# One query tile per head pair: transposes move from TensorE to VectorE blocks and transfers

## The chip, the cores and the metric

The kernel runs on one core of a Trainium2 chip. The metric is the device time of one execution in microseconds (us). All arithmetic of the reference is done on the core; the host only lays the inputs out and reads the result back.

## The reference

Attention with pooled queries, and two feed-forward layers behind it, all in float32.

```python
q_pool = q.reshape(B, H, S // 2, 2, D).mean(axis=3)          # B=2, H=8, S=1152, D=64
scores = q_pool @ k.T / sqrt(D)                              # 576 x 1152 for each head
attn = exp(scores - max) / (sum + 1e-9)
x = (attn @ v)  as (1152 tokens, 512)
x = softplus(x @ w_in) @ w_out                               # 512 -> 2048 -> 512
xn = x / rms(x) * rms_g
out = (silu(xn @ w_gate) * (xn @ w_val)) @ w_out2            # 512 -> 1536 -> 512
```

## The kernel before, in words

The 16 heads are taken as 8 pairs (`pb` 0 to 7). The 576 pooled queries of a pair are four tiles of 128 (`x` 0 to 3) and a half tile (`x` = 4) in which the 64 queries of both heads lie side by side.

For a tile and a head, `qk` (L644) multiplies queries with keys into a score bank of PSUM (128 queries by 1152 keys, six matmuls), and `softmax` (L671) finds the row maximum on VectorE (DVE, `nm`, L677) and the exponentials on ScalarE (ACT, `p`, L679). The exponentials have queries on the partitions; the product with the values needs keys there. So `flip` (L687) transposes them on TensorE (PE) against an identity, 128x128 at a time (L698): nine blocks for each head, eighteen for a tile, in five groups (4, 4, 4, 4 and 2 blocks), each of which is copied from PSUM to the SBUF tile `pt` by ACT (L318) or DVE (L320). `av` (L713) then multiplies `pt` with the values (L723, 36 matmuls) and the result is copied to `O`. When a pair is complete, `scales` (L730) makes the reciprocals of the sums, sends them through DRAM (`row`, `rdb`), and `shift` (L776) multiplies `O` by them into the homes of the attention results (`X1`), from which `arrived` prepares the operands of the first layer.

Score banks: one for each head. `p`: two buffers for each head. `pt`: two. Transposed groups and `av` share two PSUM banks `t`. Values `v` and rounded keys `kk`: one set for even and one for odd pairs.

In the main loop the PE work of a full tile x is, in this order: the first group of tile x (head A), `qk` of tile x+1 head A, the second group, `av` of the tile before, the third and fourth groups (head B), `qk` of tile x+1 head B, the last group. PE follows that order as written. For ACT, DVE, GpSimd (POOL) and the two queues that issue transfers (SP, ACTQ), the class `Plan` writes the order: each operation has engines on which it can run with an estimated duration, a latest time worked out backward from the end, and the planner places ready operations by these. On the chip each engine then runs its list in order and waits at each entry for what that entry needs.

SBUF is cut into areas (`AREAS`); `alloc` gives out columns of an area, prefers columns that no one has used, and makes a new owner wait for all operations of the old one. Beside attention, `decode` (L367) turns the weights of the first layer from 64-bit into 32-bit halves; four decodes are done during attention (`early`, L1115), each in a room of 2048 columns of area KF, whose 11330 columns also hold the homes `X1`. Two more are planned right after the attention loop, with rooms in KF or in LF; LF can be used only when attention's own tiles are done.

```python
T[0]()
qk(pb, x + 1, 0)
T[1]()
if prev:
    av(*prev)
if pb and x == 0:
    scales(pb - 1)
    shift(pb - 1)
T[2]()
T[3]()
if x < NF - 1:
    qk(pb, x + 1, 1)
T[4]()
```

Of the kernel before, what the change touches and what calls it, by code (L numbers as in the profile page):

```python
# [12 lines left out]
F32 = mybir.dt.float32  # L13
# [3 lines left out]
ALU = mybir.AluOpType  # L17
# [3 lines left out]
P = 128  # L21
B, H, S, D = 2, 8, 1152, 64
# [3 lines left out]
KC = DM // P  # L26
J1 = 2048 // P
J2 = 1536 // P
CK = S // P
NP = B * H // 2  # L30
NF = SQ // P
C = 2 * NF + 1
N = 384
# [2 lines left out]
AREAS = {"KF": 11330, "KR": 15360, "MR": 8760, "LR": 13632, "LF": 4608}  # L36
SEM = 0.1
SLACK = 1.0
WAIT = 3.5
WARM = 20  # L40
WAKE = 16
MM = N / 2400 + 0.014
# [17 lines left out]


class Op:
    __slots__ = ("fn", "opts", "lat", "deps", "after", "succ", "late", "n", "seq", "ready", "left", "start", "end", "eng")


class Plan:
# [64 lines left out]
        self.rings.setdefault((tag, bufs), []).append(b)  # L131
        return b

    def op(self, opts, fn, r=(), w=(), lat=0.0, after=()):
        o = Op()
        o.fn, o.opts, o.lat = fn, opts, lat
        o.deps, o.after, o.succ = set(), set(after), []
        o.n = len(self.ops)
        for keys, writes in ((r, False), (w, True)):
            for b, part in keys:  # L140
                assert b.live, "a freed buffer"
                o.deps |= self.before(b, part, writes)
        for keys, writes in ((r, False), (w, True)):
            for b, part in keys:
                (b.writers if writes else b.readers).setdefault(part, []).append(o)
                if not b.ops or b.ops[-1] is not o:
                    b.ops.append(o)
        o.deps.discard(o)
        self.ops.append(o)
        if opts[0][0] == "PE":  # L150
            self.pe.append(o)
        return o
# [9 lines left out]
    def order(self):  # L162
        for (tag, bufs), insts in self.rings.items():
            for x, b in enumerate(insts):
                if x >= bufs:
                    for o in b.ops:
                        o.deps.update(insts[x - bufs].ops)
                if x:
                    for o in b.ops:
                        o.after.add(insts[x - 1].ops[0])  # L170
        for b in self.placed:
            for o in b.ops:
                for p in b.prior:
                    for u in p.users:
                        o.deps.update(u.ops)
        for a, b in zip(self.pe, self.pe[1:]):
            b.after.add(a)
        for o in self.ops:
            o.deps.discard(o)
            o.after -= o.deps  # L180
            o.after.discard(o)
            o.left = len(o.deps) + len(o.after)
            for d in o.deps:
                d.succ.append((o, True))
            for d in o.after:
                d.succ.append((o, False))
        topo = [o for o in self.ops if o.left == 0]
        left = {o.n: o.left for o in self.ops}
        for o in topo:
            for s, _ in o.succ:  # L190
                left[s.n] -= 1
                if left[s.n] == 0:
                    topo.append(s)
        assert len(topo) == len(self.ops), [o.fn for o in self.ops if left[o.n]][:4]
        for o in reversed(topo):
            e, d = o.opts[0][:2]
            need = 0.0
            for s, hard in o.succ:
                if hard:
                    need = min(need, s.late - o.lat - (SEM if s.opts[0][0] != e else 0.0))  # L200
                elif e == "PE" == s.opts[0][0]:
                    need = min(need, s.late)
                else:
                    need = min(need, s.late + d)
            o.late = need - d
        self.span = -min(o.late for o in self.ops)
        return self.run()

# [64 lines left out]
def body(ctx: ExitStack, tc: tile.TileContext, kT, qT, v, w1, w1o, wg, wv, w2o, rg, outT):  # L273
    nc = tc.nc
    ctx.enter_context(tc.manual_schedule())
    engines = {"ACT": nc.scalar, "DVE": nc.vector, "POOL": nc.gpsimd}
    plan = Plan()
# [46 lines left out]

    issued = {"SP": [], "ACTQ": []}

    def load(out, src, kb, w, queue="SP", lat=2.2):
        q = nc.sync if queue == "SP" else nc.scalar
        o = op([(queue, 0.6 + max(0, kb / 220 - 0.6))], lambda e: q.dma_start(out=out(), in_=src), w=w, lat=lat,
               after=issued[queue][-1:] if len(issued[queue]) < 10 else ())  # L330
        issued[queue].append(o)
        return o
# [34 lines left out]
    def decode(srcs, combine, phase, fs, rs):  # L367
# [13 lines left out]
        def word(w, x0, x1):  # L381
            return raw()[:, x0:x1, :].rearrange("p x (f w) -> p x f w", w=2)[:, :, :, w]

        def each(t, x0, x1):
            return t()[:, x0 * DM:x1 * DM].rearrange("p (x f) -> p x f", f=DM)
# [32 lines left out]
        for w, t in ((1, b), (0, s)) if combine else ((1, b),):  # L418
            for x0, x1 in cuts:
                n = (x1 - x0) * DM  # L420
                rp = [(room, (w, x)) for x in range(x0, x1)]
                hp, lp = [(t.hi, x) for x in range(x0, x1)], [(t.lo, x) for x in range(x0, x1)]
                op([act(n)], lambda e, w=w, t=t, x0=x0, x1=x1: copy(
                    e, each(t.hi, x0, x1), word(w, x0, x1).bitcast(F32)), r=rp, w=hp)
                op([pool(n)] if phase == "exp" else [dve(n)], lambda e, w=w, t=t, x0=x0, x1=x1: tt(
                    e, each(t.lo, x0, x1), word(w, x0, x1).bitcast(F32), each(t.hi, x0, x1), ALU.subtract), r=rp + hp, w=lp)
        plan.free(room)

    class Operand:
# [110 lines left out]
    def prep(pb):  # L540
# [10 lines left out]
        def load_q(h, c, queues=("SP", "SP")):  # L551
            cut = slice(0, 2 * P) if c == 0 else slice(2 * P, 2 * SQ) if c == 1 else slice(0, 2 * SQ)
            for z in range(2):
                parts = [(qr[h], (x, z)) for x in range(2) if c in (x, None)]
                load(lambda z=z: qr[h]()[z * D:z * D + D, cut], qT[n + h][:, cut], (cut.stop - cut.start) // 4, parts, queues[z])

        for h in range(2):
            qr.append(ring("a", "p1", [P, 2 * SQ], F32, 2) if first and h else ring("e", "qr", [P, 2 * SQ]))
# [4 lines left out]
        if first:  # L563
            for c, cut, m in kcuts:
                load(lambda cut=cut: kr()[:, cut], pairs[:, cut], 192, [(kr, c)], "SP" if c else "ACTQ", (2.0, 3.1, 2.7)[c])
            load_q(1, 0)
        else:
            load(kr, pairs, 576, [(kr, None)])
        for h in range(2):
            load_q(h, 1 if first else None)  # L570
            vt = ring("ea"[pb % 2], f"v{h}{pb % 2}", [P, CK, D])
# [115 lines left out]
    def flip(pb, x, todo, halves=False):  # L687
# [19 lines left out]
        for i, j in cuts:  # L707
# [2 lines left out]
                                        t()[:, i * P:j * P].rearrange("p (c q) -> p c q", c=j - i)),  # L710
               r=[(t, None)], w=[(pt, hc) for hc in todo[i:j]])

    def av(pb, x):  # L713
        s = st[pb]
        pt = units[pb, x, 0]["pt"]
        t = tbank()
        n = P if x < NF else D

        def go(e):
            for c in range(CK):  # L720
                for h in range(2):
                    rhs = pt()[:, c, h, :] if x < NF else pt()[:, c, 0, h * D:h * D + D]
                    nc.tensor.matmul(t()[h * D:h * D + D, :n], lhsT=s["v"][h]()[:, c, :], rhs=rhs,  # L723
                                     start=(c == 0), stop=(c == CK - 1))
        op([("PE", 0.1 + CK * 0.24 * n / P)], go, r=[(pt, None), (s["v"][0], None), (s["v"][1], None)],
           w=[(t, None)])
        o = s["O"]
        op([dve(n, psum=True), act(n, False)], lambda e: copy(e, o()[:, x * P:x * P + n], t()[:, :n]), r=[(t, None)], w=[(o, x)])
# [385 lines left out]
    prep(1)  # L1114
    early = {(1, 0): [(first_pair, 0)], (3, 0): [(first_pair, 1)], (4, 0): [(first_out, 0)], (5, 0): [(first_out, 1)]}  # L1115
    prev = None
    for pb in range(NP):
        last = pb == NP - 1
        for x in range(NF + 1):
            if x == 1 and 0 < pb < NP - 1:  # L1120
                prep(pb + 1)
            for make, n in early.get((pb, x), ()):
                make(n, "exp", "KF", "KR")
            T = turn(pb, x)
            if x < NF:
                T[0]()
                qk(pb, x + 1, 0)
                T[1]()
                if prev:
                    av(*prev)  # L1130
                if pb and x == 0:
                    scales(pb - 1)
                    shift(pb - 1)
                T[2]()
                T[3]()
                if x < NF - 1:
                    qk(pb, x + 1, 1)
                T[4]()
            else:
                if not last:  # L1140
                    qk(pb + 1, 0, 0)
                T[0]()
                T[1]()
                if not last:
                    qk(pb + 1, 0, 1)
                else:
                    nb, ab, bb = make_banks(1)
                    m1_alone(0, nb)
                T[2]()
                av(*prev)  # L1150
                if last:
                    scales(pb)
            prev = (pb, x)
    op([("ACTQ", 0.6)], lambda e: nc.scalar.dma_start(out=rgs, in_=rg), after=[plan.pe[-1]])
    m1_alone(1, bb)
    av(*prev)
    spread(NP - 1, 0)
    spread(NP - 1, 1)
    Y = make_banks(0)
# [211 lines left out]
```

## Time and profile before

| | |
|---|---|
| median of 3 runs | 671.76 us (671.13 to 672.28) |
| the profiled execution | 670.88 us |
| its span, first to last instruction | 668.8 us |
| granted PE clock | full through the span |
| PE busy | 660.2 us, 99% |
| DVE, ACT, POOL busy | 72%, 59%, 19% |

The span is what the profile's rows divide up; some 2 us of the execution lie outside it. Attention fills it from the start to about 257 us, the first layer follows to about 460 us, the second runs to the end. A line such as L318, L320 or L323 is a helper's (copies, two-operand arithmetic), so its groups are told apart by the tiles they write and read.

### The profile page before, as it was taken

To read this page: it belongs to the slowest core of one execution; us is meant where nothing else is said; L and a number is where in the kernel's file an instruction comes from. 1 tells how busy PE (TensorE), PEld (TensorE's weight loads), DVE (VectorE), ACT (ScalarE), POOL (GpSimd) and SP (SyncE) were. 2 spreads that over 40 slices of the span, in tenths; PEclk is the share of its full clock that TensorE was granted. 3 is DMA by queue.
4 is the path that set the end of the run, shared out by engine and by line. 5 is a ranking of instruction groups with operands and counts; after the bars stand their busy time and mean duration, and the time that the engine had idled before them with its cause. 6 is when DMAs were issued, how large, how long until landed. Compare 5 with 4: busy or idle time off the path is not lost.

```text
span 668.8 us, 12191 instructions
## 1 busy us (share of the span) xinstructions
PE 660.2 (99%) x4947; PEld 636.8 (95%) x4947; DVE 483.3 (72%) x745; ACT 395.6 (59%) x655; POOL 130.0 (19%) x147
## 2 busy tenths in 40 slices
PE   8999999999999999999999999999999999999997
PEld 7999999999988989999999999999999999999997
DVE  8878778787777877888787566788878777752221
ACT  4988888878887775556645745456545432432231
POOL 0442634564442210000000102001011001020000
PEclk9999999999999999999999999999999999999999
DMA  7775334224240204312321130150333122101011
GB/s 194 241 211 153 104 86 119 54 83 114 84 125 1 82 2 162 113 62 107 126 84 42 64 127 2 63 189 1 127 113 139 57 71 94 33 1 48 0 48 48
DMA packets 20854, 59.77 MB, mean 89 GB/s; under 512 B 3839, under 2 KB 6206, under 8 KB 20798
## 3 DMA queue, kind: packets, MB, share of 16 engines
q1 hardware_dynamic: 20286, 58.63, 27.4%
q8 instruction: 39, 0.64, 0.4%
q10 hardware_dynamic: 512, 0.36, 0.2%
q14 instruction: 17, 0.14, 0.1%
HBM read 56.59 MB, written 2.39 MB: 88 GB/s over the span
## 4 chain that ended last, share of the span: by engine, by line
PE 93%; DVE 3%; issue 1%; ACT 1%; DMA 1%; POOL 0%; ACTq 0%; DVEq 0%; POOLq 0%
PE s L838 28%; PE s L663 11%; PE t L723 11%; PE t L698 10%; PE s L903 7%; PE s L905 7%; PE s L904 7%; PE t L838 6%; PE t L905 2%; PE t L903 2%; PE t L904 2%; PE t L1065 1%; DVE nm L677 1%; DMA kr<-in_kT_dram 1%; DVE kk L323 0%
## 5 line engine op out<-in xcount | busy, mean ns | idle before, releaser
L677 DVE TENSOR_REDUCE nm<-s 128x1 f32<-128x1152 f32 x72 | 97.7, 1357 | 21.4 <-PE s L663 21.0
L679 ACT ACTIVATE p<-s,nm 128x1152 f32<-128x1152 f32 x72 | 88.2, 1225 | 14.4 <-DVE nm L677 13.0
L698 PE MATMUL t<-ident,p 128*128 128x128 f32 x576 | 84.2, 278 | 2.3 <-ACT pt L318 1.0
L318 ACT COPY pt<-t 128x512 f32<-128x512 f32 (+2 forms) x131 | 67.1, 525 | 28.1 <-PE t L698 20.7
L723 PE MATMUL t<-pt,v 128*64 128x128 f32 (+1 forms) x1440 | 80.1, 265 | 0.0
L698 PEld LDWEIGHTS t<-ident,p 128*128 128x128 f32 x576 | 64.9, 140 | 14.6 <-issue 4.8
L723 PEld LDWEIGHTS t<-pt,v 128*64 128x64 f32 x1440 | 71.3, 137 | 7.2 <-issue 6.6
L318 ACT CAST areaLR<-areaKF 128x384 fp32r<-128x384 f32 (+2 forms) x50 | 39.1, 783 | 42.4 <-PE t L905 19.1
L318 ACT CAST areaKR<-areaKF 128x1024 fp32r<-128x1024 f32 (+3 forms) x49 | 39.0, 804 | 24.5 <-PE t L905 7.0
L838 PE MATMUL s<-areaLR,areaKR 128*128 128x384 f32 x206 | 49.9, 339 | 0.2 <-DVE areaLF L941 0.2
L838 PE MATMUL s<-areaLR 128*128 128x384 f32 x204 | 49.3, 337 | 0.0
L838 PE MATMUL s<-areaMR,areaKR 128*128 128x384 f32 x190 | 44.4, 337 | 0.4 <-DVE s L320 0.4
L323 POOL TENSOR_TENSOR kk<-kr,kk 64x384 fp32r<-64x384 f32 x40 | 39.4, 1008 | 26.9 <-ACT kk L318 15.9
L320 DVE COPY pt<-t 128x512 f32<-128x512 f32 (+2 forms) x53 | 34.1, 657 | 12.7 <-PE t L698 12.2
L838 PE MATMUL s<-areaMR,areaLR 128*128 128x384 f32 x184 | 42.1, 337 | 0.0
L401 DVE SCALAR_TENSOR_TENSOR areaKF<-areaKF 128x1024 int32<-128x1024 int32 (+1 forms) x35 | 39.4, 1127 | 1.3 <-ACT areaKF L390 0.9
L838 PEld LDWEIGHTS s<-areaLR,areaKR 128*128 128x128 f32 x206 | 37.2, 188 | 0.5 <-DVE areaLF L941 0.5
L390 ACT ACTIVATE areaKF<-areaKF 128x1024 f32<-128x1024 f32 (+1 forms) x35 | 36.7, 1048 | 0.9 <-DMA areaKF<-in_w_dram 0.9
L838 PEld LDWEIGHTS s<-areaLR 128*128 128x128 f32 x204 | 36.7, 188 | 0.0
L323 POOL TENSOR_TENSOR gl<-g,gh 128x384 fp32r<-128x384 f32 x8 | 8.2, 1030 | 143.0 <-ACT gh L318 101.0
L323 DVE TENSOR_TENSOR areaKF<-areaKF 128x256 f32<-128x256 f32 (+2 forms) x77 | 35.5, 485 | 0.8
L838 PEld LDWEIGHTS s<-areaMR,areaKR 128*128 128x128 f32 x190 | 34.0, 188 | 0.7 <-DVE s L320 0.7
(270 smaller groups left out, 1560.0 us busy)
## 6 DMA issues: line engine op xcount, KB each, us to landing
qr<-in_qT_dram SPq DMA_DIRECT2D x28, 288.0 KB, 4.5
areaKF<-in_w_dram SPq DMA_DIRECT2D x14, 512.0 KB, 6.0
areaKF<-in_w1o_dram SPq DMA_DIRECT2D x14, 512.0 KB, 3.7
areaKF<-in_w2o_dram SPq DMA_DIRECT2D x12, 512.0 KB, 3.5
areaKF<-in_wg_dram SPq DMA_DIRECT2D x11, 512.0 KB, 3.6
areaKF<-in_wv_dram SPq DMA_DIRECT2D x11, 512.0 KB
v<-in_v_dram SPq DMA_DIRECT2D x16, 288.0 KB, 3.1
kr<-in_kT_dram SPq DMA_DIRECT2D x7, 576.0 KB, 3.9
```

What stands on the lines that cost most here:

```text
L318: nc.scalar.copy(out, in_)
L323: engines[e].tensor_tensor(out=out, in0=in0, in1=in1, op=o)
L401: op([dve(n)], lambda e, x0=x0, x1=x1: nc.vector.scalar_tensor_tensor(out=word(1, x0, x1), in0=word(1, x0, x1), scalar=3, in1=word(0, x0, ...
L663: nc.tensor.matmul(sc()[:, c, :N], lhsT=q()[:, cut], rhs=k()[:, c * N:(c + 1) * N], start=(i == 0), stop=(i == len(todo) - 1))
L677: u["mx"] = op([dve(S, psum=True)], lambda e: nc.vector.tensor_reduce(out=nm(), in_=sc()[:, :, :N], axis=AX.XY, op=ALU.max, negate=True), ...
L679: o = op([("ACT", 1.42)], lambda e: nc.scalar.activation(out=pr(), in_=sc()[:, :, :N], func=AF.Exp, bias=nm(), accum_out=s["den"]()[:, col ...
L698: nc.tensor.transpose(t()[:, i * P:(i + 1) * P], pr[:, c * P:(c + 1) * P], ident)
L723: nc.tensor.matmul(t()[h * D:h * D + D, :n], lhsT=s["v"][h]()[:, c, :], rhs=rhs, start=(c == 0), stop=(c == CK - 1))
L838: nc.tensor.matmul(out, lhsT=a(k), rhs=b(k), start=start and k + i == 0, stop=stop and k + i == 3, skip_group_check=seeded)
L903: nc.tensor.matmul(o, lhsT=wh, rhs=gh(), start=first, stop=False)
L904: nc.tensor.matmul(o, lhsT=wh, rhs=gl(), start=False, stop=False)
L905: nc.tensor.matmul(o, lhsT=wl, rhs=gh(), start=False, stop=last)
```

## The change

One tile (x = 1) of the pairs 1 to 6 is no longer transposed on PE. In its place `stream` has DVE transpose the exponentials of each head in 32x32 blocks (one instruction of 128x1152 for a head) into a tile `turned`, and 16 transfers of 32 partitions by 576 floats (2304 bytes) each, all on SP, carry the blocks to the partitions where they belong, in a tile `moved`. `av` of such a tile is taken one pair later, in tile x = 2 of the next pair (for pair 6: in tile 1 of pair 7), reads `moved` with a strided pattern (four runs of 32 floats), and `shift` of the pair follows it there. `turned` and `moved` have one buffer each (2304 columns of area KF each, held until the end of attention). The homes `X1` (4608 columns) are given out before the loop. The latest times of some operations are set earlier: 5 us for the low halves of decodes during attention, 4 us for the loads of queries and keys (all but the first pair's).

```diff
+HURRY = 5.0
+EARLY = 4.0
+G = 32
+GW = 2 * CK * G
+STREAMED = {(pb, 1) for pb in range(1, NP - 1)}
...
-            o.late = need - d
+            o.late = need - d - o.hurry
...
                 op([pool(n)] if phase == "exp" else [dve(n)], lambda e, w=w, t=t, x0=x0, x1=x1: tt(
-                    e, each(t.lo, x0, x1), word(w, x0, x1).bitcast(F32), each(t.hi, x0, x1), ALU.subtract), r=rp + hp, w=lp)
+                    e, each(t.lo, x0, x1), word(w, x0, x1).bitcast(F32), each(t.hi, x0, x1), ALU.subtract), r=rp + hp, w=lp,
+                   hurry=HURRY if phase == "exp" else 0.0)
...
-            load(kr, pairs, 576, [(kr, None)])
+            load(kr, pairs, 576, [(kr, None)], hurry=EARLY)
...
+    def stream(pb, x):
+
+        turned, moved = rings["turned"](), rings["moved"]()
+        units[pb, x, 0]["pt"] = moved
+        for h in range(2):
+            pr = units[pb, x, h]["p"]
+            op([("DVE", 1.37, 1)], lambda e, h=h, pr=pr: nc.vector.transpose(
+                turned().rearrange("p (b h c j) -> p h c b j", b=P // G, h=2, j=G)[:, h],
+                pr().rearrange("p k (c b j) -> p (k c) b j", b=P // G, j=G)), r=[(pr, None)], w=[(turned, h)])
+        for b in range(P // G):
+            for a in range(P // G):
+                op([("SP", 0.62)], lambda e, a=a, b=b: nc.sync.dma_start(
+                    out=moved()[b * G:(b + 1) * G, a * GW:(a + 1) * GW], in_=turned()[a * G:(a + 1) * G, b * GW:(b + 1) * GW]),
+                   r=[(turned, 0), (turned, 1)], w=[(moved, (a, b))], lat=4.0)
...
-                    rhs = pt()[:, c, h, :] if x < NF else pt()[:, c, 0, h * D:h * D + D]
+                    if (pb, x) in STREAMED:
+                        rhs = pt().rearrange("p (b h c j) -> p h c b j", b=P // G, h=2, j=G)[:, h, c]
+                    else:
+                        rhs = pt()[:, c, h, :] if x < NF else pt()[:, c, 0, h * D:h * D + D]
...
+    late = []
+    X1.of("alone", KC * N)
+    for t in X1.two:
+        for k in range(2):
+            X1.of((k, t))
+    for tag in ("turned", "moved"):
+        rings[tag] = plan.around(tag, 2 * S, 1, "KF")
...
+            if (pb, x) in STREAMED:
+                stream(pb, x)
+                qk(pb, x + 1, 0)
+                av(*prev)
+                qk(pb, x + 1, 1)
+                prev = late.pop() if late else None
+                late.append((pb, x))
+                continue
...
                 if prev:
                     av(*prev)
+                    if prev in STREAMED:
+                        shift(pb - 1)
                 if pb and x == 0:
                     scales(pb - 1)
+                    if (pb - 1, 1) not in STREAMED:
+                        shift(pb - 1)
+                T[2]()
+                if x == 1 and late:
+                    av(*late.pop())
                     shift(pb - 1)
-                T[2]()
...
     av(*prev)
+    for tag in ("turned", "moved"):
+        for b in rings.pop(tag).bases:
+            plan.free(b)
```

## Rows read from the trace of the kernel before

**Rows 1.** The page: busy time and share of the span by engine.
```profile
PE 660.2 (99%) x4947; PEld 636.8 (95%) x4947; DVE 483.3 (72%) x745; ACT 395.6 (59%) x655; POOL 130.0 (19%) x147
```
**Rows 2.** Busy time by stretch: start:end, length, engines, PE clock, DMA share, GB/s.
```profile
20.00:50.00 30.00, 29.79 (x323) 27.45 (x325) 23.25 (x37) 25.48 (x41) 13.81 (x17) 1.00 0.75 223
...
140.00:170.00 30.00, 29.79 (x323) 27.28 (x321) 23.21 (x32) 24.77 (x46) 16.87 (x21) 1.00 0.35 99
...
260.00:275.00 15.00, 15.00 (x88) 15.00 (x87) 13.34 (x20) 10.87 (x17) 1.02 (x1) 1.00 0.65 238
```
**Rows 3.** The chain that ended last, 100 to 136 us: start, length, what.
```profile
104.24 1.20 PE t L723 x36
...
114.13 0.66 PE t L698 x6
114.78 1.05 PE s L663 x6
115.84 0.44 PE t L698 x4
116.27 2.12 PE t L723 x36
118.39 1.05 PE t L698 x8
119.44 1.05 PE s L663 x6
120.49 0.65 PE t L698 x6
...
134.37 1.20 PE t L723 x36
```
**Rows 4.** Timeline from 119.8 us, part of it: scores, maximum, exponentials, copies.
```profile
119.81 0.68 PE L663 MATMUL s<-kk,qlB 128*128 128x384 f32 x3
...
120.64 1.36 DVE L677 TENSOR_REDUCE nm<-s 128x1 f32<-128x1152 f32 x1
120.74 1.08 ACT L318 COPY pt<-t 128x256 f32<-128x256 f32 x2
...
122.04 1.23 ACT L679 ACTIVATE p<-s,nm 128x1152 f32<-128x1152 f32 x1 [0.22 <-DVE nm L677]
```
**Rows 5.** Groups by shape, 28 to 247 us: count, busy us, mean ns.
```profile
L318 ACT COPY pt<-t 128x512 f32<-128x512 f32 x91 | 52.3, 586 | 24.0 <-PE t L698 19.1 <-PE t L1065 2.8
...
L320 DVE COPY pt<-t 128x512 f32<-128x512 f32 x41 | 27.7, 689 | 9.9 <-PE t L698 9.6
...
L318 ACT COPY pt<-t 128x256 f32<-128x256 f32 x25 | 9.3, 372 | 2.3 <-PE t L698 1.3
...
L320 DVE CAST kh<-kr 128x1152 fp32r<-128x1152 f32 x5 | 3.8, 751 | 0.8 <-PE s L663 0.8
```
**Rows 6.** Line L723 alone, semaphore waits in PE's queue: ns min/median/max, first and last.
```profile
L723 PEldq EVENT_SEMAPHORE  x8: 51/51/51, 19.1 to 229.0; - x8
```
**Rows 7.** Timeline of SP, 109 to 140 us and 195 to 330 us, parts.
```profile
113.93 2.46 SPq L756 DMA_DIRECT2D rdb<-row  x4
...
132.28 0.35 SPq L329 DMA_DIRECT2D kr<-in_kT_dram  x1
...
226.71 1.06 SPq L329 DMA_DIRECT2D areaKF<-in_w_dram  x2
258.47 0.80 SPq L329 DMA_DIRECT2D areaLF<-in_w_dram  x2
```
**Rows 8.** Timeline of POOL and of PE, 195 to 260 us, parts.
```profile
235.06 1.31 POOL L323 TENSOR_TENSOR areaKR<-areaKF,areaKR 128x512 fp32r<-128x512 f32 x1 [2.80 <-ACT areaKR L318]
...
257.07 0.42 PE L903 MATMUL s<-gh,areaKR 128*128 128x384 f32 x1
```

More of the change, by code (lines that the diff above doesn't have):

```diff
@@ L62 @@
 class Op:
-    __slots__ = ("fn", "opts", "lat", "deps", "after", "succ", "late", "n", "seq", "ready", "left", "start", "end", "eng")
+    __slots__ = ("fn", "opts", "lat", "deps", "after", "succ", "late", "n", "seq", "ready", "left", "start", "end", "eng", "hurry")
 class Plan:
@@ L132, in ring, with op @@
         return b
-    def op(self, opts, fn, r=(), w=(), lat=0.0, after=()):
+    def op(self, opts, fn, r=(), w=(), lat=0.0, after=(), hurry=0.0):
         o = Op()
-        o.fn, o.opts, o.lat = fn, opts, lat
+        o.fn, o.opts, o.lat, o.hurry = fn, opts, lat, hurry
         o.deps, o.after, o.succ = set(), set(after), []
@@ L325, in body, with load @@
     issued = {"SP": [], "ACTQ": []}
-    def load(out, src, kb, w, queue="SP", lat=2.2):
+    def load(out, src, kb, w, queue="SP", lat=2.2, hurry=0.0):
         q = nc.sync if queue == "SP" else nc.scalar
-        o = op([(queue, 0.6 + max(0, kb / 220 - 0.6))], lambda e: q.dma_start(out=out(), in_=src), w=w, lat=lat,
+        o = op([(queue, 0.6 + max(0, kb / 220 - 0.6))], lambda e: q.dma_start(out=out(), in_=src), w=w, lat=lat, hurry=hurry,
                after=issued[queue][-1:] if len(issued[queue]) < 10 else ())
@@ L554, in load_q @@
                 parts = [(qr[h], (x, z)) for x in range(2) if c in (x, None)]
-                load(lambda z=z: qr[h]()[z * D:z * D + D, cut], qT[n + h][:, cut], (cut.stop - cut.start) // 4, parts, queues[z])
+                load(lambda z=z: qr[h]()[z * D:z * D + D, cut], qT[n + h][:, cut], (cut.stop - cut.start) // 4, parts, queues[z], hurry=0.0 if first else EARLY)
         for h in range(2):
```

## The prediction

> **What bounds the kernel now.** I read the engines' busy shares first: PE is busy for 660.2 of 668.8 us [rows 1], so almost no time is left in which PE waits, and a change pays only by what it takes from PE's list or costs by the waits it puts there. A busy PE can still hide a wait in a stage, so I read the stretches next: during attention PE is busy 29.79 of each 30 us while DVE and ACT have 23.2 and 24.8 us of work in the same 30 [rows 2]. Two engines that are busy four fifths each and never hold PE up are near their limit but not at it; the reader should keep both halves of that. Third, the chain of waits through one pair shows that attention's end is set by PE alone, piece after piece, in the order written in the loop [rows 3]. A full tile is the stretch from 114.13 to 120.49: transposes 0.66 + 0.44 + 1.05 = 2.15 us, scores 1.05 + 1.05 = 2.10 us, product with the values 2.12 us, together 6.37 us. A pair is the distance between two of its half-tile products, 134.37 - 104.24 = 30.1 us [rows 3].
>
> **What is removed.** In six tiles the eighteen transposes go: 6 x 2.15 = 12.9 us of PE's list [rows 3]. With them go four copies of 512 columns and one of 256: on ACT 4 x 0.586 + 0.372 = 2.72 us for a tile, on DVE at 0.689 somewhat more [rows 5].
>
> **What is added on DVE.** Two block transposes of 128x1152 a tile. The trace has no DVE transpose. From below: DVE casts 128x1152 in SBUF in 0.751 us [rows 5]. From above: twice the row maximum over 1152 elements, which takes 1.36 us [rows 4], so 2.7 us. I take 1.36 us, the same engine with as many float32 elements read once each; the fast cast is nearer in place (SBUF) but a block transpose is less like a copy. So 2.72 us for a tile, as much as the copies that went. For a pair DVE and ACT together then still have 23.2 + 24.8 = 48.0 us per 30, of which 60 were on offer; a pair shortens to 27.95 us, 55.9 on offer, so their joint share rises from 80% to 86%.
>
> The Trainium skill speaks against this edit: the page "VectorE: DVE Perf Modes", section "Rules for kernel authors", says to transpose 128x128 on TensorE if a PSUM destination will do, and its section "The three transpose paths" gives 311 ns for a 128x128 bf16 block transpose on DVE. An estimate from that page is 9 x 311 ns = 2.8 us for a head. No row here has the operation; by the page's figure the sum would come out beyond the slow rival below, at about 684 us.
>
> **Where PE can now wait.** The streamed tile leaves PE only scores, product, scores: 1.05 + 2.12 + 1.05 = 4.22 us [rows 3]. The question is whether the softmax of tile 2 keeps up. From the end of the scores (120.49 [rows 3]) maximum and exponentials end at 122.04 + 1.23 = 123.27 [rows 4], 2.78 us later when both engines are at hand; I add 0.05 for the hand-over and use 2.83.
> Head A of tile 2: between its scores and its first transposes PE has the product and head B's scores, 2.12 + 1.05 = 3.17 us. Slack 0.34 us.
> Head B: between its scores and its transposes stand 0.44 + 1.05 + 0.44 us and a product of 2.12 us, 4.05 us. Slack 1.22 us. In pair 1 there is no older product to put there, so 1.93 us stand against 2.83: a wait of 0.9 us, once.
> The product inside the streamed tile needs all copies of tile 0. Its last group is now followed by 1.05 us of scores only, where transposes stood as well (0.66, 0.44 more). A copy of 256 columns (0.37) fits if ACT or DVE is free; behind a maximum (1.36) or an exponential (1.23) it is about 0.7 us late [rows 4, 5].
> For these two tight places I take 0.3 us a tile, between nothing and about 1.0: 6 x 0.3 = 1.8 us.
>
> **Semaphores.** The product of a streamed tile waits for 16 transfers. In the trace the product's line shows one extra wait instruction of 51 ns in PE's queue for each of the 8 pairs [rows 6], where fresh values arrive. Bounds: nothing, if PE's queue runs ahead while scores are computed; 16 x 0.051 = 0.82 us a tile if it can't. I take half, 0.4: 6 x 0.4 = 2.4 us.
>
> **Strided reads of the product.** No row has them. Bounds: nothing, or the product doubled (2.12 us more). I take nothing: the matmuls still read each value once and in runs.
>
> **Transfers.** 16 x 32 x 2304 bytes are 1.2 MB a pair. PE was as busy in the stretch with a DMA share of 0.75 as in the one with 0.35 [rows 2], so I charge no contention. On SP an issue takes 0.35 to 2.46 / 4 = 0.6 us [rows 7], so 16 take 5.6 to 9.8 us of a pair of 28, and they can't start before the older product has released `moved`. Queued behind them on SP are the next loads of keys, queries and values, `row`, `rdb`, and decode loads. Keys for pair 5 are loaded at 132.28, about when pair 4 begins, a pair ahead of their use [rows 7]; 9.8 us late would still be in time. The cover is that pair-long lead; without it the 9.8 us would fall on the next pair's scores. `av` comes a pair later than the transfers, so they have 20 us and more. I charge nothing.
>
> **Rooms and the later shift.** With 4608 columns for `X1` and 4608 for `turned` and `moved`, 2114 of KF's 11330 are left, so the four early decodes share one room. The last low half of them was done at 235.06 + 1.31 and first used at 257.07 [rows 8], 20.7 us ahead; the decodes were already spread in time, so I charge nothing. KF then has no unused room for the first decode after attention either, whose load was issued at 226.71; it will likely go to LF, whose first load came at 258.47 [rows 7]. Then a few us of DVE work move into a stage where DVE has 13.34 of 15 us to do [rows 2]: from nothing to about 4 us of PE waiting (three passes over 1024 columns at the maximum's rate [rows 4], 3.6 us, an estimate), and I take nothing, because its first use is two steps of the layer later. `shift` moves by a tile and a half inside a pair; its engines are the ones counted above.
>
> **The sum.** 12.9 - 0.9 - 1.8 - 2.4 = 7.8 us saved. The profiled execution took 670.88 us and becomes 663.1; the median of the runs is 0.88 above it, so the prediction is 664.0 us. Differences under 0.2% (1.3 us) I count as no change, about what a measurement here can tell.
>
> **Rivals.**
> *The whole gain* (0.18). PE's queue swallows the semaphore waits and the copies come in time: 12.9 - 0.9 = 12.0 us, 659.8 us. For it speaks that PE hardly waited at 80% of DVE and ACT; against it the 0.34 us of slack.
> *Gain eaten by waits* (0.16). Every wait at its upper bound: 12.9 - 0.9 - 4.9 - 6 x 1.0 = 1.1 us, 670.7 us. The place is the product in the streamed tile and in the tile that reads `moved`. Half of this case I count as no change.
> *Slower: a DVE transpose stands ahead of the maximum* (0.11). DVE runs its list in order. If a transpose of duration d precedes each maximum of tile 2, head A is late by d - 0.34 and head B by d - 1.22. That costs more than the 2.15 us gained when 2d > 3.71, so from d = 1.86 us on. At 2.05, midway between my value and the upper bound, the tile loses 2.54 - 2.15 = 0.39 us: 6 x 0.39 + 0.9 = 3.2 us, 675.0 us; at 2.8 it would lose 1.91, about 684. For it: the maxima leave DVE little room in 4.22 us. Against it: the transposes can wait until tile 3 needs the buffers of `p`, and the nearest row says 1.36.
> *SP or the rooms run late* (0.03). Loads behind the transfers, or a decode late after attention: 4 us or more in one place and again in others, about 675 us. Against it stand the leads above.
> The forecast itself has 0.52, with 661.5 to 667.5 us as its own range. Faster by over 0.2%: 0.52 + 0.18 + half of 0.16, about 0.79; within: 0.08; slower: 0.13. The range reaches to the whole gain below and into the eaten one above, 659.5 to 671.5; what it leaves out is the slower cases and a little beyond either end.
>
> **What the profile will show.** Right: L698 with 108 matmuls fewer and a tile of about 4.2 us of PE in each of pairs 1 to 6; transposes of 1.36 us on DVE; 96 more issues on SP; PE still busy 97% or more in attention; the end of attention some 8 us earlier and the layers unchanged. Wrong: PE idle before L698 in tile 2 put down to the exponentials (slower rival), wait instructions at the product that open gaps near 0.8 us (eaten gain), products longer than 2.12 us (strided reads), or PE waiting for keys, `moved` or a decoded weight (SP, rooms).

## The result and the profile after

The changed kernel takes 660.74 us (660.63 to 660.83) against 671.63 us before: a ratio of 0.9837, 95% interval 0.982 to 0.9854, 10.9 us less. It lies inside the whole range of 659.5 to 671.5, but 3.3 us under the predicted 664.0 and under the forecast's own 661.5 to 667.5; nearest to it is the first rival, the whole gain, with 659.8 us. The profiled execution took 660.63 us, its span 658.5 us.

The page's busy times answer to [rows 1]:

```profile
PE 648.5 (98%) x4839; PEld 625.8 (95%) x4839; DVE 490.5 (74%) x744; ACT 391.1 (59%) x642; POOL 128.7 (20%) x143
```

PE is still the engine that is busy throughout; it has 108 matmuls fewer (4947 before), the transposes of six tiles. DVE is the one engine whose work grew.

The stretches answer to [rows 2], in the same columns:

```profile
0.00:20.00 20.00, 17.52 (x91) 15.35 (x92) 16.56 (x38) 10.58 (x19) 2.38 (x9) 0.91 0.73 203
20.00:50.00 30.00, 29.79 (x328) 27.23 (x328) 23.69 (x38) 24.85 (x40) 13.44 (x18) 1.00 0.48 138
50.00:80.00 30.00, 28.82 (x304) 26.29 (x301) 25.91 (x33) 23.68 (x43) 8.42 (x11) 1.00 0.44 110
...
140.00:170.00 30.00, 29.61 (x314) 27.03 (x313) 25.58 (x32) 22.79 (x40) 14.01 (x18) 1.00 0.58 149
```

DVE has gone from 23.2 to 25.6 of 30 us in the stretch from 140 us, PE from 29.8 to 29.6. The stretch from 50 us holds pair 1, where PE is idle for more than a microsecond: the tile without an older product.

The chain that ended last, through the streamed tile of pair 3 and between two half-tile products, answers to [rows 3]:

```profile
99.67 1.20 PE t L747 x36
...
103.17 1.06 PE s L669 x6
104.23 2.12 PE t L747 x36
106.34 1.25 PE s L669 x6
107.59 0.44 PE t L704 x4
108.03 1.07 PE s L669 x6
...
109.54 2.12 PE t L747 x36
111.65 1.08 PE t L704 x8
...
127.66 1.20 PE t L747 x36
```

The streamed tile is the stretch from 103.17 to 107.59, 4.42 us; 4.22 were predicted, 6.37 is a tile with transposes. The extra 0.2 us is in the second scores (1.25 us where six matmuls else take 1.05): PE's load side is idle for 0.17 us behind a product. The kernel before has the same gap behind its product, there ahead of eight transposes (the first line is from before, the second from after):

```profile
118.32 0.88 PEld L698 LDWEIGHTS t<-ident,p 128*128 128x128 f32 x8 [0.17 <-issue]
106.27 0.48 PEld L669 LDWEIGHTS s<-kk,qhB 128*128 128x128 f32 x3 [0.17 <-issue]
```

That is why eight transposes took 1.05 us before where four took 0.44. The gap is not new, and it did not go with the transposes.

A pair lasts 127.66 - 99.67 = 27.99 us, against 30.1. The product at 109.54 is the one that reads `moved`, in 2.12 us like any other: the strided reads cost nothing.

The starts of the first and the last half-tile product, from the same view of each run, give attention without its start (us):

| | pair 0's | pair 7's | between |
|---|---|---|---|
| before | 44.42 | 255.42 | 211.00 |
| changed | 44.80 | 245.03 | 200.23 |
| no tile streamed | 44.60 | 256.75 | 212.15 |
| three pairs | 45.41 | 254.96 | 209.55 |
| the block transposes first | 44.59 | 253.13 | 208.54 |

The change shortens this stretch by 10.77 us. What follows the last product until the end of the span lasts 413.4 us before and 413.5 after, so the layers are unchanged. The last three rows belong to runs described below.

DVE's timeline over the same tile shows where the block transposes stand:

```profile
102.98 2.64 DVE L683 TENSOR_REDUCE nm<-s 128x1 f32<-128x1152 f32 x2 [0.20 <-PE s L669]
105.54 1.37 DVE L725 STREAM_TRANSPOSE areaKF<-p 128x1152 f32<-128x1152 f32 x1
...
107.63 1.36 DVE L683 TENSOR_REDUCE nm<-s 128x1 f32<-128x1152 f32 x1 [0.54 <-PE s L669]
109.14 1.36 DVE L683 TENSOR_REDUCE nm<-s 128x1 f32<-128x1152 f32 x1 [0.15 <-PE s L669]
```

One takes 1.37 us (1.36 was taken). Head A's comes after the maximum that tile 2 needs (the second of the two at 102.98) and before the next can start, whose scores are done only at 107.59; head B's stands at 112.88, behind two more maxima.

Line L747 alone, the semaphore waits of the products, answers to [rows 6], and line L730 shows the transfers (ns min/median/max):

```profile
L747 PEldq EVENT_SEMAPHORE  x32: 51/51/51, 19.5 to 219.1; - x32
```
```profile
L730 SPq DMA_DIRECT2D areaKF<-areaKF x96: 507/589/1841, 56.9 to 211.0; - x96
```

24 wait instructions more than before for six products: four each, not sixteen.

### The profile page after: what moved, and what is told of

Its sections match the earlier page's. It is cut to its first block, busy times and chain, and to the rows that moved or that the text cites. A ratio compares the mean times of both kernels' runs of the same rounds, so it can differ in the third digit from the quotient of the medians.

```text
span 658.5 us, 12113 instructions
## 1 busy us (share of the span) xinstructions
PE 648.5 (98%) x4839; PEld 625.8 (95%) x4839; DVE 490.5 (74%) x744; ACT 391.1 (59%) x642; POOL 128.7 (20%) x143
## 4 chain that ended last, share of the span: by engine, by line
PE 94%; DVE 3%; ACT 1%; DMA 0%; issue 0%; DVEq 0%; ACTq 0%
PE s L862 28%; PE s L669 12%; PE t L747 11%; PE t L704 8%; PE s L927 7%; PE s L929 7%; PE s L928 7%; PE t L862 6%; PE t L929 2%; PE t L927 2%; PE t L928 2%; PE t L1089 1%; DVE nm L683 1%; ACT pt L323 0%; DMA qr<-in_qT_dram 0%
## 5 line engine op out<-in xcount | busy, mean ns | idle before, releaser
L704 PE MATMUL t<-ident,p 128*128 128x128 f32 x468 | 69.4, 279 | 3.4 <-ACT pt L323 1.1
L747 PE MATMUL t<-pt,v 128*64 128x128 f32 (+1 forms) x1224 | 67.0, 263 | 0.0
L747 PEld LDWEIGHTS t<-pt,v 128*64 128x64 f32 x1224 | 59.6, 137 | 6.7 <-issue 6.0
L704 PEld LDWEIGHTS t<-ident,p 128*128 128x128 f32 x468 | 53.0, 140 | 13.6 <-issue 3.3
L323 ACT COPY pt<-t 128x512 f32<-128x512 f32 (+2 forms) x99 | 49.8, 520 | 26.1 <-PE t L704 20.9
L328 POOL TENSOR_TENSOR kk<-kr,kk 64x384 fp32r<-64x384 f32 x42 | 41.5, 1015 | 37.2 <-ACT kk L323 33.2
L325 DVE COPY pt<-t 128x512 f32<-128x512 f32 (+1 forms) x55 | 34.8, 650 | 9.8 <-PE t L704 9.6
L328 POOL TENSOR_TENSOR qs<-qr 128x224 f32<-128x224 f32 (+1 forms) x39 | 23.2, 621 | 54.8 <-DVE qm L605 28.6
```

The source lines that it names most:

```text
L323: nc.scalar.copy(out, in_)
L328: engines[e].tensor_tensor(out=out, in0=in0, in1=in1, op=o)
L704: nc.tensor.transpose(t()[:, i * P:(i + 1) * P], pr[:, c * P:(c + 1) * P], ident)
```

## The experiments

Ratios are to the kernel before, measured beside each run, with 95% intervals. The changed kernel's is 0.9837. Differences in us are to the median of the changed kernel, 660.74 us; worked out from the ratios they come out the same within 0.8 us.

**No tile streamed.**

```diff
-STREAMED = {(pb, 1) for pb in range(1, NP - 1)}
+STREAMED = set()
```


> The changed kernel with no tile streamed: the homes are still given out first, turned and moved still hold their columns, and the latest times are still set earlier, but all tiles are transposed on TensorE as before. Theory A (the gain is what left TensorE's list, nothing else): no change from the kernel before, 671.6 us within 1.3. Rival P (part of the gain comes from the homes and from the planner's other order): 668 us or less.


672.74 us, 1.0015 (1.0005 to 1.0025). The homes, the columns held and the earlier latest times alone gain nothing; they cost about 1 us, in attention (212.15 against 211.00 us in the table above). The whole gain belongs to the streamed tiles.

**Three pairs.**

```diff
-STREAMED = {(pb, 1) for pb in range(1, NP - 1)}
+STREAMED = {(pb, 1) for pb in (1, 3, 5)}
```


> Only pairs 1, 3 and 5 have a streamed tile; each product is then taken in tile 1 of the next pair, so tile 2 has no older product in all three pairs. Theory A with a wait of 0.9 us wherever tile 2 has no product: 3 x 1.95 - 3 x 0.9 = 3.2 us saved, 668.5 us. If that hole costs nothing: 3 x 1.95 = 5.9 us saved, 665.8 us.


670.79 us, 0.9993 (0.9982 to 1.0005), 2.3 us slower than expected and not told apart from the kernel before. PE's waits show the hole at its expected size, three times 1.07 us (in us: total, times, longest):

```profile
PE t L704 <- ACT p L685: 3.2, 3, 1.4
```

The changed kernel has one such wait:

```profile
PE t L704 <- ACT p L685: 0.9, 1, 0.9
```

So a streamed tile pays its full 1.95 us only when an older product stands in the next tile. The trace shows most of the rest. Attention is 1.45 us shorter than before (209.55 against 211.00 in the table above), not 3.2: of 3 x 1.95 = 5.85 us the holes take 3.2, and PE's other waits (copies, keys, queries) add up to 4.0 us against 2.8 before. The first half-tile product also comes 1.0 us later than before, and what follows the last one lasts 1.0 us longer; why is not shown.

**The block transposes first.** Two dependencies make each maximum of tile 2 wait for the same head's transpose.

```diff
                 qk(pb, x + 1, 0)
+                units[pb, x + 1, 0]["mx"].deps.add(blocks[pb, x][0])
                 av(*prev)
                 qk(pb, x + 1, 1)
+                units[pb, x + 1, 1]["mx"].deps.add(blocks[pb, x][1])
```


> The changed kernel with one order forced: on VectorE each block transpose stands ahead of the maximum of the same head of tile 2. By the slacks of the prediction (0.34 us for head A, 1.22 for head B) a transpose of 1.37 us makes each of six tiles 1.03 + 0.15 us longer: 7.1 us, 667.8 us, still under the kernel before. If the slacks are larger than worked out (rival): under 663 us. If VectorE's order is what bounds the stage: 672 us or more.


670.01 us, 0.9983 (0.9974 to 0.9992): 9.3 us slower than the changed kernel where 7.1 was expected. In attention it is 8.3 us (208.54 against 200.23 in the table above), 1.4 us a tile where 1.18 was expected; the rest comes behind it. Most of the gain is lost with two dependencies that change DVE's order, though the planner wrote the other lists anew as well. PE's wait for exponentials, 0.9 us in the changed kernel, is now:

```profile
PE t L704 <- ACT p L685: 6.0, 5, 1.9
...
PE s L669 <- ACT p L685: 0.9, 2, 0.7
```

Four of these waits stand ahead of head A's first transposes in tile 2, 1.04, 1.52, 0.75 and 0.76 us, where the slack gave 1.03. In all, waits for exponentials are up by 6.0 of the 8.3 us, waits for copies to `pt` by 1.2.

**Nothing in the transposes' place.** The block transposes and the transfers are left out; `moved` is filled once with a constant, so the streamed products are those of a constant.

```diff
-        turned, moved = rings["turned"](), rings["moved"]()
+        moved = rings["moved"]
...
-            op([("DVE", 1.37, 1)], lambda e, h=h, pr=pr: nc.vector.transpose(
...
-                op([("SP", 0.62)], lambda e, a=a, b=b: nc.sync.dma_start(
...
+    op([("POOL", 6.5)], lambda e, m=rings["moved"]: nc.gpsimd.memset(m(), 0.5), w=[(rings["moved"], None)])
```


> The changed kernel without the block transposes and the transfers: the tile moved is filled once with a constant and read by all six products, so VectorE loses 16.4 us of work and SP 96 issues, and the products of the streamed tiles are those of a constant. Theory A (both are hidden): 660.7 us within 0.6. Rival D (VectorE or the waits for 16 transfers still cost): 1.5 us or more under the changed kernel, 659.2 us or less.


661.46 us, 0.9851 (0.9838 to 0.9864), no faster than the changed kernel. Its order lost 2.4 us at the start, where PE waited for rounded queries, so the stretch from pair 0's half-tile product to pair 6's is the better measure (rows of the chain, first this run's, then the changed kernel's):

```profile
45.92 1.20 PE t L737 x36
...
213.18 1.20 PE t L737 x36
```
```profile
44.80 1.20 PE t L747 x36
...
212.18 1.20 PE t L747 x36
```

167.26 us against 167.38 us. In this order the transposes and the 96 transfers are hidden entirely.

**Each transpose twice.**

```diff
-        for h in range(2):
+        for h in (0, 1, 0, 1):
```


> The changed kernel with each block transpose done twice, so VectorE gets 16.4 us more in pairs 1 to 6, and each wait for a transpose is longer by up to 2.7 us. Theory A (VectorE has room, and its list puts the maxima first): 660.7 to 663 us. Rival D (VectorE is the bound as soon as it has about 3 us more a pair): 668 us or more; by the slow rival of the prediction, with 2.74 us ahead of each maximum, 684 us.


677.95 us, 1.0105 (1.0089 to 1.0121): 17 us slower than the changed kernel for 16.4 us more of DVE. Theory A fails here. DVE reaches 27.1 to 27.8 of 30 us from 110 to 200 us, and PE waits for exponentials (4.7 us), key halves (3.7) and queries (1.8 and 1.5). What was hidden at 25.6 of 30 is no longer hidden 2 us higher. Room and order aren't told apart here: in pairs 1 and 2 both of head A's transposes stand ahead of the maximum of tile 2's head B.

**Both latest times as before, then each alone.**

```diff
-HURRY = 5.0
-EARLY = 4.0
+HURRY = 0.0
+EARLY = 0.0
```


> The changed kernel with the two shifts of latest times set to 0. The run without streaming was 1.1 us slower than the kernel before (672.74 us), so some part of the change other than streaming costs about that. If it is these shifts: 659.7 us. If they were needed so that low halves and loads are not late beside the transfers (rival): 662 us or more. Indifferent: 660.7 within 0.6.


675.93 us, 1.0063 (1.0045 to 1.0081): slower than the kernel before, 15.2 us worse than the changed kernel, as the rival has it.

> The changed kernel with the 5 us shift of the decodes' low halves set to 0 and the 4 us shift of the loads kept. Theory R (the decodes share one room, run late without the shift, and hold up the change of ACT's table behind attention): 670 us or more, as with both shifts at 0 (675.9 us). Rival E (the loads' shift was what mattered there): 661 to 662 us.


667.75 us, 0.994 (0.9928 to 0.9953), 7.0 us worse: between the two, in the direction of theory R. The pairs run as in the changed kernel (half-tile products at 44.80 there and 45.56 here, the last at 245.03 and 245.50). The loss is all behind them: PE's first product of the first layer waits 4.54 us for an operand made from the softplus, whose table ACT loads at 249.56, right behind the last decode's activation, against 241.96 in the changed kernel.

ACT's and PE's timeline at that place:

```profile
248.88 0.67 ACT L395 ACTIVATE areaKF<-areaKF 128x512 f32<-128x512 f32 x1
249.56 1.28 ACT L1358 ACT_TABLE_LOAD   x1
251.94 0.69 PE L927 MATMUL s<-gh,areaKR 128*128 128x384 f32 x1 [4.54 <-ACT gh L323]
```

> The changed kernel with the 4 us shift of the loads set to 0 and the 5 us shift of the low halves kept. Theory R: 660.7 to 662 us. Rival E (loads of queries and keys queue behind the 16 transfers without it, and the scores of a next pair wait): 664 us or more.


668.13 us, 0.9949 (0.9936 to 0.9961), 7.4 us worse: rival E. On SP the transfers of pair 5 (174.73 to 186.16) now stand ahead of all loads of pair 7's queries. Those of its first head come at 186.26; in the changed kernel they came at 163.13 and 169.31, ahead of the transfers. Their sums (`qs`, one buffer) start at 191.44 in place of 175.59, those of the second head at 208.17 in place of 191.48, and the first scores of pair 7's second head wait:

```profile
212.98 1.39 PE L669 MATMUL s<-kk,qhB 128*128 128x384 f32 x3 [2.62 <-DVE kk L328]
...
215.04 3.85 PE L747 MATMUL t<-pt,v 128*64 128x128 f32 x36
```

That wait and the slower product behind it (last section) are 4.3 of the 7.4 us; a copy that comes late in pair 5, at 169.14, adds 1.6. The two losses, 7.0 and 7.4 us, add up to nearly the 15.2 us of both.

**Homes given out later.**

```diff
-    X1.of("alone", KC * N)
-    for t in X1.two:
-        for k in range(2):
-            X1.of((k, t))
```


> The changed kernel with the homes X1 given out one by one as in the kernel before, so that the early decodes find more than one room, and a home can lie where a decode's room was. Theory R (the one room is the tight place that the shift of 5 us guards): no slower than the changed kernel, 659.5 to 661.3 us. Rival H (a home then waits for a decode, which is why they are set aside): 663 us or more.


668.02 us, 0.9945 (0.9932 to 0.9957), 7.3 us worse: theory R fails, more room is no help. But the profile doesn't show rival H's wait either. The chain in pair 4 shows what the run with the transposes first forced, come about by the planner's other order: a block transpose ahead of the maximum (start, length, what):

```profile
146.71 1.36 DVE areaKF L725
148.08 1.25 DVE nm L683
...
149.41 1.32 ACT p L685 x2
...
150.78 0.67 PE t L704 x4
```

Whether a home's wait for a decode turned the order is left open.

**More tiles, and the hole filled.** Pair 0 too; then all pairs, with the last product ahead of the last half-tile product; then the changed kernel with pair 0's half-tile product moved into pair 1's hole.

```diff
+STREAMED = {(pb, 1) for pb in range(NP - 1)}
...
+STREAMED = {(pb, 1) for pb in range(NP)}
...
     m1_alone(1, bb)
+    av(*late.pop())
     av(*prev)
...
+                if pb == 1:
+                    av(0, NF)
+                    shift(0)
```


> Pair 0 is streamed too, seven tiles in all; the tile 2 without an older product is now that of pair 0, and pair 1 gets the product of pair 0. Theory A: one tile more, 1.95 us saved, 658.8 us. Rival: in pair 0 the conversions of the first operands and the decode loads leave VectorE and SP no room, 661 us or more.


665.02 us, 0.991 (0.9895 to 0.9924), 4.3 us worse than six tiles: the rival. In the stretch from 20 to 50 us, mostly pair 0, PE is busy 26.47 of 30 us, where the changed kernel has 29.79. The chain goes through SP: ten of pair 0's transfers, then the load of pair 2's queries, for which DVE's list stands still, and behind it PE:

```profile
35.82 0.59 SPq L730
...
37.09 4.73 DMA qr<-in_qT_dram
...
41.95 0.29 DVE qs L328
```

> All eight pairs are streamed; the last pair's streamed product is taken after the loop, right ahead of the last half-tile product. Theory A: two tiles more than the changed kernel, 3.9 us saved, 656.8 us. Rival: the transfers of pair 7 can start only after the product of pair 6 and hold the end of attention, where nothing else stands behind them: 659 us or more.


672.28 us, 1.001 (0.9998 to 1.0022). The end of attention is lost too: the first layer's first product starts at 253.77, against 246.68 in the changed kernel, after PE waited 3.71 us for the scales of pair 7. The rival is right in its place, SP, but it isn't `moved` that comes late. Behind the last transfer (issued by 240.34) and the rows of pair 6's scales SP issues the weights of a decode; DVE's list stands at that decode for 6.97 us, and the copies of pair 7's scales (`rdb`) stand behind it:

```profile
239.75 0.59 SPq L730
...
244.06 4.58 DMA areaKF<-in_w1o_dram
...
250.89 1.66 DVE rdb L325 x2
```

In the changed kernel the last such load before the end of attention starts by 234.7.

> The changed kernel with the half-tile product of pair 0 taken not in tile 0 of pair 1 but behind the streamed tile's second scores, where tile 2 of pair 1 lacked an older product. Theory: the wait of 1.1 us there goes (the same wait cost 1.07 us a pair in the run with three pairs), 659.6 us. Rival: the planner's other order costs as much, 660.7 us or more.


664.88 us, 0.9896 (0.9881 to 0.9911), 4.1 us worse, as the rival has it. In pair 1 the 0.9 us wait for exponentials is gone, but 1.0 us of waits for copies stand in its place. In pair 7 PE waits 1.04 us at 221.93, which the chain follows back through a decode's cast on ACT and its arithmetic on DVE, and 0.68 us for a copy; the product behind them takes 3.85 us in place of 2.19 (last section). The new order of the other engines costs more than the filled hole brings.

## Why the prediction was right, and where it was not

In the main the first rival came true, the whole gain, which had 0.18: the queue takes the semaphore waits and the copies come in time. The direction and what bounds the kernel were right; the forecast of 7.8 us charged two terms that measured nothing (1.8 and 2.4 us) and took 1.2 us too much as removed. That these partly cancel, and leave only 3 us, is luck. The rival's 659.8 us holds the same 1.2 us too much.

**What bounds, and what is removed.** Right. PE sets the end of attention before and after, and the gain is its shortened list. The term of 12.9 us was too large by 1.2: a streamed tile saves 6.37 - 4.42 = 1.95 us, not 2.15. The 1.05 us that I read as eight transposes held the gap of 0.17 us behind the product, and that gap stays. So 11.7 us.

**Pair 1.** 0.9 us predicted, 0.9 measured in the changed kernel's waits, and 1.07 a time with three holes. 11.7 - 0.9 = 10.8 us, against 10.77 between the half-tile products and 10.9 by the medians. The cost of about 1 us that the run without streaming shows has no place in this sum; whether it is paid in the changed kernel too is not shown.

**Tight places, 1.8 us.** Oversized: next to nothing. The waits for exponentials in the changed kernel are the one of pair 1, and PE's waits for copies are as before (in us: total, times, longest; two lines before, two after):

```profile
PE t L698 <- ACT pt L318: 1.0, 5, 0.2
PE t L698 <- DVE pt L320: 1.0, 3, 0.4
```
```profile
PE t L704 <- ACT pt L323: 1.1, 5, 0.3
PE t L704 <- DVE pt L325: 1.0, 3, 0.3
```

The slack of 0.34 us sufficed with the maxima first in DVE's list; with the transposes first it didn't.

**Semaphores, 2.4 us.** Oversized: it measured nothing. Four wait instructions in place of sixteen, and PE's gap ahead of the product is the 0.17 us that other products have.

**DVE's transposes.** 1.37 us measured, 1.36 taken. The Trainium skill's figure ("VectorE: DVE Perf Modes", "The three transpose paths", 311 ns for 128x128 in bf16) gave an estimate of 2.8 us for a head; the trace disagrees with that estimate: 1.37 us for nine blocks' worth of float32 in one instruction, 0.152 us for each 128x128. A single one in bf16 is in no run here. The Trainium skill's rule (same page, "Rules for kernel authors") to keep 128x128 transposes on TensorE doesn't hold in this kernel, where TensorE is the engine that sets the time: six tiles that left it saved 10.9 us. The slow rival's mechanism is real, as the run with the transposes first shows: its threshold was worked out as 1.86 us for each transpose, and at 1.37 the run lost 9.3 us where the formula gives 7.1.

**Transfers and rooms, charged nothing.** The number was right for the kernel as changed, and the reason given was wrong. I argued from leads in the profile of before, a pair for the loads and 20.7 us for the decodes, as if they would last; and I gave the two shifts of latest times no term at all. Without both the same leads are gone and the kernel is slower than before: 7.4 us without the shift of the loads, 7.0 us without that of the decodes. The rival "SP or the rooms run late" had the right places, and 0.03 was far too little for how near it lay: in the run without the loads' shift, with pair 0 and with all pairs a load stands behind transfers on SP and PE ends up waiting. With the rooms it is less clear: giving the homes out later, which leaves the decodes more rooms, was slower. The first decode after attention did not go to LF, as I thought likely; it stayed in KF (ACT's activation of it starts at 232.13).

**The profiled start.** The profiled execution gained 10.25 us, less than the medians; 0.4 us of the difference is in the first 20 us, where the granted clock was 0.91 (the first product of pair 0 starts at 20.25, 19.89 before).

What stays open: in every experiment, how much is the edit and how much the order that the planner happened to write. Each edit rewrote the lists of four engines, and no run held them fixed. It weighs most with the homes given out later and the filled hole.

## What to carry to other kernels

When one engine is busy all the time, work that leaves it is worth its stretch of the chain (1.95 us a tile), not its busy time or its instructions' durations (272 ns a transpose), and the engines that take the work over must be asked for order, not only for room: DVE had a third of a microsecond to spare, and two instructions the other way round took back most of the gain. Leads that a profile shows (loads a pair ahead, decodes 20 us ahead) are results of the old order; an added 10 us on the same queue can use them up, so the priorities that keep them are terms of the sum. Stop where the slack ends: six tiles saved 10.9 us, seven some 6, eight nothing.

## What the runs showed of the hardware

After some of PE's waits the granted clock fell to the lower level for some microseconds, so that the wait cost more than its length. In the run with the loads' shift at 0, by stretch (start:end, length, busy times, clock, DMA share, GB/s):

```profile
209.00:213.00 4.00, 1.38 (x12) 1.10 (x10) 3.31 (x6) 3.94 (x6) 1.51 (x2) 1.00 0.69 184
213.00:215.00 2.00, 1.94 (x8) 1.22 (x8) 1.97 (x6) 1.47 (x3) 0.00 (x0) 1.00 0.98 353
215.00:217.00 2.00, 2.00 (x22) 1.96 (x22) 1.94 (x5) 0.90 (x2) 0.00 (x0) 0.54 1.01 221
217.00:219.00 2.00, 2.00 (x22) 1.83 (x19) 0.29 (x2) 1.23 (x3) 0.00 (x0) 0.61 0.51 160
219.00:223.00 4.00, 4.00 (x59) 3.73 (x58) 3.60 (x6) 1.37 (x3) 0.24 (x1) 1.00 0.34 121
```

PE was busy 1.38 of 4 us, then worked on at full clock for some 2 us, and then ran mostly at the lower level (1.2 GHz of 2.4) while it was fully busy: the product there took 3.85 us in place of 2.19 on its timeline, 1.7 us on top of a wait of 2.62. With the low halves' shift at 0 the clock was 0.50 from 250 to 256 us, in and behind the wait of 4.54 us. With the filled hole shorter waits did it: PE was busy 0.96 of 2 us from 220, then 1.32 of 2 us, and the clock was 0.50 from 224 to 226 us. The changed kernel, whose waits in attention are under 1 us each and stand apart, shows 1.00 in every stretch of attention after the first 20 us.
